# A gated long convolution and a gated feed-forward on one core: four homes in on-chip memory, the first half's output stage inside the second half's spectra, and the feed-forward's opening in another order

## The chip, the core and the metric

One NeuronCore of one Trainium2 chip. The five engines that the text names are TensorE (PE in the profile, with its weight loads as PEld), VectorE (DVE), ScalarE (ACT), GpSimd (POOL) and SyncE (SP), which here only issues transfers. The time is device microseconds of one execution. A program whose time is compared is run several times and its median is taken.

## What is computed

A block with adaptive layer norm, over 2048 rows of 448 channels, all in float32:

```python
mod = silu(c) @ w_mod                       # six vectors of 448: sa, ca, ga, sb, cb, gb
h = layernorm(x) * (1 + ca) + sa            # x is q
kv = causal_conv4(k, shift_k) * v           # per channel, 4 taps
y = irfft(rfft(kv, 4096) * rfft(ssm_k, 4096))[:2048] + kv * ssm_D
x = x + ga * h * y
h = layernorm(x) * (1 + cb) + sb
x = x + gb * ((sigmoid(h @ w_gate) * (h @ w_up)) @ w_down)     # 448 -> 1792 -> 448
```

## The kernel before

**Layout.** A tile has 128 partitions. The 2048 rows are 16 groups of 128. The 448 channels are two halves of 224 (`h` = 0 and 1 in names such as `y0_3`, `av[:, h]`, `gate(h, i)`).

**The convolution** is done by Fourier transforms written as matmuls. `stage1_k` and `stage1_v` (lines 171 and 183) do a first small transform, the VectorE transposes 32 by 32 blocks in place (`turn`, line 167: eight turns for a half), `stage2_k` and `stage2_v` (229 and 259) do the second. `stage2_v(h, between)` runs eight steps `n`. Each step multiplies on PE into an accumulator `s2v`, multiplies that on the VectorE by the kernel's spectrum `ak` and by its copy with swapped halves `kx` (which a transfer `load_kx` brings, two buffers), and transforms the two products `m` back on PE (`inv`, into `sa`), from where ACT copies them over the spectrum in `av`. `inv` runs one step late. After it `between(n)` emits whatever else is to stand there. When a half's eight steps and its eight turns are done, `stage_out(h, i)` (299) makes output rows of four groups, eight matmuls per `i` into an accumulator `y`, `y_copy` brings it out of PSUM, and `gate(h, i, y, eng)` (314) multiplies with the first norm's result `G` and adds to the residual `x1`. The half 0 is gated on POOL, half 1 on the VectorE. The six modulation vectors are made on the way: a transfer `mod_load`, three POOL instructions `mod_sum`, a PE sum over partitions `mod_use`.

**The feed-forward** holds each float32 operand as a high and a low part, and multiplies high x high, low x high and high x low. Its 1792 hidden columns are 7 groups of 256 (`j`), the rows 4 blocks of 512 (`n`), so there are 28 blocks `(j, n)`, each with two halves `f`. `gate_up(j, n, f)` (630) is 22 matmuls: 11 for the gate (`s` = 0), 11 for the up product (`s` = 1), into one `gu` accumulator, of which there are two. ACT and VectorE make the hidden values `hh` and `hl` from it. `down(j, n, hs, e)` (651) is 12 matmuls into an accumulator `d`, and the VectorE adds `d` to `x1`. The down product of a block is emitted during the next block: after `gate_up(.., 0)` comes `down(*prev, 0)`, after `gate_up(.., 1)` comes `down(*prev, 1)`. A weight group `j` arrives by six transfers of raw weights `r` (`load_w(j, k)`: k = 0, 1 gate, 2, 3 up, 4, 5 down), and `split_hi` (ACT) and `split_lo` (VectorE) make the two parts in `wt`; the down weights are first multiplied by `gb` on POOL.

**The second norm** of a block of rows: statistics (`ln2_stats`, two of four row groups on ACT with `sq`, the others on the VectorE), `ln2_end` (square root on ACT, reciprocal on VectorE), `norm_rows(n)` (601, the VectorE writes normed rows `xn`), `norm_turn(n, t)` (611, four PE transposes into `pt`, ACT and VectorE make the high and low parts in `xt`).

**What sets the order.** Nothing is scheduled by a tool: `tc.manual_schedule()` (450) keeps the order in which the Python emits, and each engine runs its own list in that order. Waits follow from the tiles: an instruction waits for the writers of what it reads, and a tile that takes a place in memory waits for the readers of the tile that was there. Around the change the order is set by `during0` and `during1` (548 and 563, the `between` of the two halves), by the lines 577 to 683, and by the tables `jobs` and `ends` (708 to 727): `jobs[p, f]` is emitted inside `gate_up` of block number `p`, `ends[p, f]` behind the down product. Blocks 0 to 7 are `(0,0), (1,0), (0,1), (1,1), (0,2), (0,3), (1,2), (1,3)`. All transfers below are issued by SP in order.

**Places in memory.** Pool `big` has the tags `ak` (two buffers: the kernel's spectra of both halves, later the weights `wt` of two groups) and `av` (one buffer: the spectra of `kv` of both halves, later `xt`). Raw weights have two buffers of their own (`pr`, line 426).

## Time and profile before

| | us |
|---|---|
| median of 3 executions | 667.43 (665.19 to 670.30) |
| the profiled execution | 668.59 |
| its span, first to last instruction | 666.8 |
| last matmul of the second half's spectra ends, about | 177 |
| last turn of the second half ends, about | 187 |
| first feed-forward matmul | 208.14 |
| from here on PE has no gap | 300.26 |

How to read it: the page gives each engine's busy time and the span in 40 slices of 16.7 us. A timeline row is start, duration, engine, line, operation, tiles, shape, and in brackets the idle time of that engine before it with what ended it. Durations overlap at their ends where an engine is pipelined, so the time from one start to the next is the price of an instruction in a row of them. `x8` at the end of a row is a count of merged instructions; a float32 matmul shows as two.

### The profile page before, as it was taken

What the parts mean: (1) busy time and instruction counts of PE and PEld (TensorE: products, weight loads), DVE (VectorE), ACT (ScalarE), POOL (GpSimd) and SP (SyncE); (2) the same over time, 40 slices, a digit from 0 to 9 for tenths busy, and PEclk for the clock granted to TensorE, in tenths of its full rate; (3) what the DMA queues carried; (4) which work ended last, traced back from release to release, by engine and by line L of the source; (5) the groups of instructions that cost most, each with busy time, mean ns of one, the idle gap of its engine ahead of it and who ended that gap; (6) DMA issues with size and microseconds to landing.
All of it is one profiled execution on the core that took longest, in us unless ns stands there. A gap on an engine that the chain in (4) does not pass through costs nothing.

```text
span 666.8 us, 7048 instructions
## 1 busy us (share of the span) xinstructions
PE 597.1 (90%) x2764; PEld 457.5 (69%) x2764; DVE 350.1 (53%) x402; ACT 251.1 (38%) x436; POOL 131.5 (20%) x101
## 2 busy tenths in 40 slices
PE   8597795998847677789999999999999999999997
PEld 6355442433435366678888888888888888888886
DVE  0859985989998644433224443344334433442233
ACT  5575577974535476341113222222212212221110
POOL 1224286689890100000001001000000100000000
PEclk9898997999986789899999999999999999999999
DMA  8931288773210200000001111001101010100112
GB/s 296 282 83 54 82 293 206 190 183 88 68 46 15 90 32 1 0 1 0 1 1 59 32 32 43 17 16 30 46 1 32 28 32 16 31 15 0 56 55 111
DMA packets 23765, 44.44 MB, mean 67 GB/s; under 512 B 10354, under 2 KB 12916, under 8 KB 23604
## 3 DMA queue, kind: packets, MB, share of 16 engines
q1 hardware_dynamic: 23668, 43.98, 23.0%
q8 instruction: 22, 0.36, 0.2%
q14 instruction: 11, 0.09, 0.0%
q0 software_dynamic: 64, 0.01, 0.0%
HBM read 32.98 MB, written 3.67 MB: 55 GB/s over the span
## 4 chain that ended last, share of the span: by engine, by line
PE 65%; DVE 13%; DMA 8%; ACT 7%; issue 3%; POOL 3%; SPq 0%; POOLq 0%; DVEq 0%; ACTq 0%
PE gu L639 39%; PE d L662 20%; DVE av L169 4%; PE s2k L234 3%; DVE acc L208 2%; DMA kT<-in_kT_dram 2%; DMA wm<-in_wmod_dram 2%; PE pt L618 2%; POOL wm L333 1%; ACT full L620 1%; DMA early<-in_ssm_dram 1%; DVE wt L443 1%; POOL wm L334 1%; DMA r<-in_wu_dram 1%; ACT xt L624 1%
## 5 line engine op out<-in xcount | busy, mean ns | idle before, releaser
L639 PE MATMUL gu<-xt,wt 128*128 128x512 f32 x1232 | 299.1, 398 | 3.6 <-ACT wt L437 3.6
L639 PEld LDWEIGHTS gu<-xt,wt 128*128 128x128 f32 x1232 | 236.2, 192 | 52.2 <-ACT wt L437 4.0
L644 DVE TENSOR_TENSOR sg<-sg,gu 128x512 f32<-128x512 f32 x56 | 38.4, 686 | 198.8 <-ACT sg L643 198.8
L662 PE MATMUL d<-wt,hh 128*128 128x448 f32 x448 | 127.4, 366 | 1.9 <-ACT sq L372 1.9
L643 ACT ACTIVATE sg<-gu 128x512 f32<-128x512 f32 x56 | 33.4, 597 | 252.5 <-PE gu L639 252.5
L662 PEld LDWEIGHTS d<-wt,hh 128*128 128x128 f32 x448 | 84.0, 188 | 11.9 <-ACT sq L372 2.4
L436 POOL TENSOR_TENSOR r<-r,gbrow 128x448 f32<-128x448 f32 x14 | 16.0, 1147 | 374.1 <-DMA r<-in_wd_dram 339.6
L662 PE MATMUL d<-wt,hl 128*128 128x448 f32 x224 | 81.8, 365 | 0.0
L663 DVE TENSOR_TENSOR x<-x,d 128x896 f32<-128x896 f32 x56 | 60.5, 1081 | 2.4 <-PE d L662 2.4
L648 DVE TENSOR_TENSOR hl<-sg,hh 128x512 fp32r<-128x512 f32 x56 | 39.7, 708 | 39.1 <-ACT hh L647 39.1
L169 DVE STREAM_TRANSPOSE av<-av 128x896 f32<-128x896 f32 x32 | 57.8, 1875 | 2.4 <-POOL wm L335 2.4
L647 ACT ACTIVATE hh<-sg 128x512 fp32r<-128x512 f32 x56 | 35.4, 631 | 45.3 <-DVE sg L644 45.3
L662 PEld LDWEIGHTS d<-wt,hl 128*128 128x128 f32 x224 | 42.1, 188 | 3.3
L618 PE MATMUL pt<-ident,xn 128*128 128x128 f32 x64 | 13.9, 336 | 22.8 <-ACT xt L624 10.5
L443 DVE TENSOR_TENSOR wt<-r,wt 128x512 fp32r<-128x512 f32 (+1 forms) x42 | 32.5, 789 | 2.8 <-ACT wt L437 2.8
L169 DVE STREAM_TRANSPOSE ak<-ak 128x896 f32<-128x896 f32 x16 | 28.1, 1815 | 9.7 <-ACT ak L181 9.7
L234 PE MATMUL s2k<-ak,w 128*128 128x448 f32 x64 | 27.1, 578 | 6.7 <-ACT acc L206 6.5
L274 PE MATMUL sa<-m,wa 128*64 128x448 f32 x64 | 28.0, 553 | 5.3 <-ACT av L276 3.4
L288 PE MATMUL s2v<-av,w 128*128 128x448 f32 x64 | 28.8, 576 | 1.7 <-ACT ak L235 1.7
L618 PEld LDWEIGHTS pt<-ident,xn 128*128 128x128 f32 x64 | 8.5, 162 | 29.0 <-ACT xt L624 11.8
L437 ACT ACTIVATE wt<-r 128x512 fp32r<-128x512 f32 (+1 forms) x42 | 24.7, 600 | 9.4 <-DMA r<-in_wu_dram 9.4
L275 PE MATMUL sa<-m,wa 128*64 128x448 f32 x64 | 27.5, 552 | 0.0
(121 smaller groups left out, 569.4 us busy)
## 6 DMA issues: line engine op xcount, KB each, us to landing
kx<-ak SPq DMA_DIRECT2D x32, 224.0 KB, 4.1
wm<-in_wmod_dram SPq DMA_DIRECT2D x12, 392.0 KB, 4.4
v<-in_v_dram SPq DMA_DIRECT2D x8, 448.0 KB, 9.1
x<-in_q_dram SPq DMA_DIRECT2D x4, 896.0 KB, 9.5
r<-in_wg_dram SPq DMA_DIRECT2D x14, 256.0 KB, 2.7
r<-in_wu_dram SPq DMA_DIRECT2D x14, 256.0 KB, 2.7
out_dram<-x SPq DMA_DIRECT2D x8, 448.0 KB, 2.5
r<-in_wd_dram SPq DMA_DIRECT2D x14, 224.0 KB, 2.5
```

Of the source, the lines that this page charges most:

```text
L169: DVE.transpose(x, x)
L234: PE.matmul(pt[:, b, :D], w2, a[:, j + 2 * b:j + 2 * b + 2], start=True, stop=True)
L288: PE.matmul(pt[:, b, :D], w2, a[:, j + b * nj // 2:j + (b + 1) * nj // 2, cs], start=True, stop=True)
L443: DVE.tensor_sub(lo, r, hi)
L618: PE.transpose(pt[:, i * P:(i + 1) * P], xn[:, i, t * P:(t + 1) * P], ident)
L639: PE.matmul(pgu[:, s], w[:, t, f * P:(f + 1) * P], x[:, xs], start=i == 0, stop=i == len(ops) - 1)
L643: ACT.activation(sg, pgu[:, 0], AF.Sigmoid)
L644: DVE.tensor_mul(sg, sg, pgu[:, 1])
L647: ACT.activation(hh, sg, AF.Copy)
L648: DVE.tensor_sub(hl, sg, hh)
L662: PE.matmul(pt[:, i, :D], h[:, (2 * e + i) * P:(2 * e + i + 1) * P], w[:, f], start=m == 0, stop=m == len(ops) - 1)
L663: DVE.tensor_add(x1[:, g:g + 2], x1[:, g:g + 2], rows(pt))
```

## The change

**Places.** `big` now has four tags with one buffer each. `k0` and `k1` hold the kernel's spectra of the halves, `a0` and `a1` those of `kv`. Later `k0` holds `tmp` (16 x 224 columns for copies of `y`, and seven places of 512 columns for raw weights), then rows 2 and 3 of the norm's result (`xt1`); `a0` holds `xt0` (rows 0 and 1); `k1` and `a1` hold the weights of even and odd groups. Later raw weights use the four `in` buffers. `stage1_v` copies each accumulator out with two ACT instructions of 448 elements, one for each half, where it was one of 896.

**Second half's spectra.** `during1` has the raw weights of group 0 loaded (three at n = 5, three at n = 6) and, at n = 5, 6, 7, `stage_out(0, 0..2)` with copy and gates; `(0, 3)` follows behind. The last two `mod_sum` stand in `during0`, their `mod_use` at n = 0 and 1. Raw weights 0 to 5 of group 0 need no buffer to come free.

**Feed-forward's opening.** Groups 0 and 1 have their raw weights in `tmp`. Only one of four statistics is on ACT for the first two row blocks. `norm_rows(n)` for n > 0 is on ACT. `norm_turn` does eight transposes at once, and the copies (`norm_split`) are separate. The norm work that stood in `jobs` is spread by `turns` and a new `ends`. `down` always uses the accumulator `y` (it alternated between `sa` and `y`); norm turns of n > 0 use `sa`.

```diff
 def stage1_v(k):
-            ACT.activation(d[:, :, g], rows(pt).rearrange("p s (h c) -> p s h c", h=2), AF.Copy)
+            for h in range(2):
+                ACT.activation(av[h].rearrange("p (s j) c -> p s j c", s=2)[:, :, g], pt[:, :, h * C:h * C + C], AF.Copy)
...
 def during0(n):
+        if n in (4, 5):
+            mod_sum(n + 6)
...
+    tmp = big.tile([P, 32 * C], F32, tag="k0", name="tmp")
 def during1(n):
-        if n < 2:
-            mod_sum(n + 10)
         if n < 5:
             next(gating)
-        if n in (3, 5):
-            mod_use(10 + n // 4)
+        if n < 2:
+            mod_use(10 + n)
...
+        if n in (5, 6):
+            for k in range(3):
+                load_raw(0, 3 * (n - 5) + k, raw(3 * (n - 5) + k))
+        if n >= 5:
+            gate(0, n - 5, y_copy(0, n - 5, stage_out(0, n - 5, "y")), POOL)
...
-    for k in range(2):
-        load_w(0, k)
-    for i in range(4):
-        if i < 3:
-            turn(av[:, 1], 2 * i + 2)
-            turn(av[:, 1], 2 * i + 3)
-        if i > 1:
-            split_hi(0, i - 2)
-        gate(0, i, y_copy(0, i, stage_out(0, i, "sa" if i % 2 else "y")), POOL)
-    y1 = [stage_out(1, i, tag) for i, tag in ((0, "y"), (1, "t"), (2, "t"))]
-    for k in range(2):
-        split_lo(0, k)
-        load_w(0, 2 + k)
-        split_hi(0, 2 + k)
+    for i in range(3):
+        turn(av[1], 2 * i + 2)
+        turn(av[1], 2 * i + 3)
+        if i == 0:
+            gate(0, 3, y_copy(0, 3, stage_out(0, 3, "y")), POOL)
+    new_w(0)
+    for k in range(4):
+        split_hi(0, k)
+    y1 = [stage_out(1, i, tag) for i, tag in enumerate(("sa", "t", "t", "y"))]
+    for k in range(3):
+        split_lo(0, k)
     gate(1, 0, y1[0], DVE)
...
-        pt = two("y" if e else "sa", f"d{j}_{g}")
+        pt = two("y", f"d{j}_{g}")
...
-    ln2_stats(0, 1, 2, 3, act=(0, 1))
-    yc = y_copy(1, 1, y1[1])
-    for k in (2, 3):
-        split_lo(0, k)
-        load_w(0, 2 + k)
-    ln2_end(0)
+    yc = [y_copy(1, 1, y1[1])]
+    ln2_stats(0, 1, 2, 3, act=(0,))
+    ln2_end(0, 1)
+    new_w(1)
+    split_lo(0, 3)
+    for k, at in enumerate((6, 0, 1, 2)):
+        load_raw(1, k, raw(at))
+    yc += [y_copy(1, i, y1[i]) for i in (2, 3)]
     norm_rows(0)
-    for t in range(4):
-        norm_turn(0, t)
...
+    norm_turn(0, 0, "sa")
+    norm_turn(0, 2, "y")
+    norm_split(0, 0)
+    norm_split(0, 2)
+    gate(1, 1, yc[0], DVE)
+    ln2_stats(4, 5, 6, 7, act=(4,))
+    for k in range(2):
+        split_w(1, k)
+    ln2_end(4, 1)
...
+    turns = {(1, 1, 0): (1, 0), (1, 1, 1): (1, 2), (2, 1, 0): (2, 0), (3, 0, 0): (2, 2), (3, 1, 0): (3, 0), (4, 0, 0): (3, 2)}
+    ends = {(0, 0): [splits_of(1, 2, 3), splits_of(0, 4, 5)],
+            (0, 1): [lambda: norm_rows(1), lambda: gate(1, 2, yc[1], DVE)],
+            (1, 0): [lambda: gate(1, 3, yc[2], DVE), lambda: load_raw(1, 4, raw(0)), lambda: load_raw(1, 5, raw(6))],
+            (1, 1): [stats_of(2), splits_of(1, 4, 5), lambda: xts.append(big.tile([P, 2, 7, 512], F32R, tag="k0", name="xt1"))],
+            (2, 0): [lambda: norm_rows(2)],
+            (2, 1): [stats_of(3)],
+            (3, 0): [lambda: norm_rows(3)],
```

**How rows move, first place:** PE's list in the last steps of the second half's spectra. `s2v1_6` is the forward product of step 6, `sa1_5` an inverse product of step 5, `y0_0` the first output product of half 0. Before:

```order
L288 MATMUL s2v1_6_1152<-av_276,w2_76 128x448 x2
L274 MATMUL sa1_5_1159<-m1_5_0_1136,wa_84 64x448
...
L288 MATMUL s2v1_7_1166<-av_276,w2_76 128x448 x2
L274 MATMUL sa1_6_1173<-m1_6_0_1155,wa_84 64x448
...
L275 MATMUL sa1_7_1180<-m1_7_1_1170,wa_84 64x448
L306 MATMUL y0_0_1200<-av_276,wb_85 64x224 x8
L306 MATMUL y0_1_1215<-av_276,wb_85 64x224 x8
```

Now:

```order
L305 MATMUL y0_0_1170<-av0_276,wb_85 64x224 x8
L287 MATMUL s2v1_6_1185<-av1_277,w2_76 128x448 x2
L273 MATMUL sa1_5_1192<-m1_5_0_1157,wa_84 64x448
...
L305 MATMUL y0_1_1202<-av0_276,wb_85 64x224 x8
L287 MATMUL s2v1_7_1214<-av1_277,w2_76 128x448 x2
L273 MATMUL sa1_6_1221<-m1_6_0_1188,wa_84 64x448
...
L305 MATMUL y0_2_1228<-av0_276,wb_85 64x224 x8
```

Three groups of eight output products now stand ahead of forward and inverse products of the other half: `y0_0` ahead of `s2v1_6`, `y0_1` ahead of `s2v1_7`, `y0_2` ahead of `sa1_7`.

**Second place:** ACT's list where it makes the high part `wt1` of group 1's down weights. `sg` and `hh` are hidden values, `full` and `xt` the norm's parts, `sq` statistics, `rstd` the square roots. Before, in block 1, `(1, 0)`:

```order
L381 ACTIVATE rstd_91<-mv_93,eps_82 128x2 x2
L643 ACT_TABLE_LOAD
L643 ACTIVATE sg1_0_0_1553<-gu1_0_0_1497 128x512
L647 ACTIVATE hh1_0_0_1556<-sg1_0_0_1553 128x512
L437 ACTIVATE wt1_1403<-r1_4_1467 128x448
L437 ACTIVATE wt1_1403<-r1_5_1471 128x448
```

Now, at the end of block 1 and the start of block 2, `(0, 1)`:

```order
L635 ACTIVATE full1_3_1585<-pt1_2_1572,cols_89 128x512
L639 ACTIVATE xt0_1318<-pt1_2_1572,cols_89 128x512
L657 ACTIVATE sg1_0_1_1589<-gu1_0_1_1532 128x512
L661 ACTIVATE hh1_0_1_1592<-sg1_0_1_1589 128x512
L371 ACTIVATE sq8_1610,mv_93<-x1_701 128x448
...
L372 ACTIVATE sq9_1613,mv_93<-x1_701,mv_93 128x448
L381 ACT_TABLE_LOAD
L381 ACTIVATE rstd_91<-mv_93,eps_82 128x2 x2
L440 ACTIVATE wt1_1336<-tmp_1027 128x448 x2
L657 ACT_TABLE_LOAD
L657 ACTIVATE sg0_1_0_1656<-gu0_1_0_1633 128x512
```

The high part of group 1's down weights stands behind four statistics, a table load and two square roots; the first product that reads it is `down(1, 0, .., 0)`, at the end of the first half of block 2. Before, it stood right behind `hh1_0_0`, a whole half-block earlier.

More of the change, by code (lines that the diff above doesn't have):

```diff
@@ L103, in quad @@
     def quad(tag, bufs, name, parts=P):
-        return (rot if tag == "in" else late["rb"]).tile([parts, 4, C], F32, tag=tag, bufs=bufs, name=name)
+        return (rot if tag == "in" else late["pg"] if tag == "G" else late["rb"]).tile([parts, 4, C], F32, tag=tag, bufs=bufs, name=name)
     def whole(t):
@@ L484, in adaln_conv_glu_kernel @@
         load_k(ct, kb)
-    av = big.tile([P, 2, 32, C], F32, tag="av", name="av")
+    av = [big.tile([P, 32, C], F32, tag=f"a{h}", name=f"av{h}") for h in range(2)]
     for k in range(4):
@@ L548, in during0 @@
     def during0(n):
-        turn(av[:, 1], n)
+        turn(av[1], n)
         if n < 5:
@@ L691, in stats_of @@
         return run
-    def turns_of(n, t0, tag):
-        def run():
-            for t in range(t0, t0 + 2):
-                norm_turn(n, t, tag)
-        return run
     def splits_of(j, *ks):
```

136 lines of the change are left out of this document (63 added, 73 removed).

## Prediction

> **What bounds the kernel now.** I read the page's slices first, then windows by stage, then the chain and the timelines.
>
> ```profile
> span 666.8 us, 7048 instructions
> PE   8597795998847677789999999999999999999997
> 190.00:210.00 20.00, 11.63 (x67) 8.53 (x64) 16.71 (x24) 9.10 (x18) 10.66 (x6) 0.67 0.17 48
> 230.00:250.00 20.00, 14.06 (x55) 10.67 (x55) 10.58 (x20) 13.67 (x25) 2.22 (x2) 0.83 0.14 47
> 350.00:660.00 310.00, 310.00 (x1422) 266.61 (x1421) 117.53 (x157) 66.72 (x114) 11.50 (x10) 1.00 0.10 31
> 300.43 5.00 PE gu L639 x22
> 305.43 2.43 PE d L662 x12
> 307.86 5.00 PE gu L639 x22
> 292.75 0.45 PE pt L618 x4
> 208.14 12.09 PE L639 MATMUL gu<-xt,wt 128*128 128x512 f32 x44
> 223.79 5.44 PE L639 MATMUL gu<-xt,wt 128*128 128x512 f32 x11 [3.56 <-ACT wt L437]
> ```
>
> In a window the columns are length, then busy time of PE, PE's weight loads, VectorE, ACT and POOL, the granted clock, the share and rate of the transfers. From 350 to 660 PE is busy without a gap at clock 1.00, and it has been since 300.26: a half-block costs 5.00 + 2.43 = 7.43 us. That stretch can't change, so the end comes earlier by as much as PE gets there earlier. In 190 to 250 PE is neither full nor at full clock. By 300.26 PE has done 8 gate-and-up halves, 6 down halves and 12 groups of four norm transposes: 8 x 5.00 + 6 x 2.43 + 12 x 0.45 = 60.0 us of work in 300.26 - 208.14 = 92.1 us. So the opening loses 32.1 us. The two things to forecast are when the first product starts, and what the opening loses now.
>
> **Second half's spectra.** Here the VectorE sets the pace, row behind row.
>
> ```profile
> 163.59 3.71 DVE L169 STREAM_TRANSPOSE av<-av 128x896 f32<-128x896 f32 x2
> 169.06 1.18 DVE L290 TENSOR_TENSOR m<-s2v,ak 128x896 f32<-128x896 f32 x1
> 174.75 12.21 DVE L169 STREAM_TRANSPOSE av<-av 128x896 f32<-128x896 f32 x7
> 165.92 1.67 PE L288 MATMUL s2v<-av,w 128*128 128x448 f32 x4
> 176.93 6.22 PE L306 MATMUL y<-av,wb 128*64 128x224 f32 x64
> ```
>
> The change adds a wait. `y0_0` needs all turns of half 0, done at 163.59 + 3.71 = 167.3. Behind it on PE stands `s2v1_6`, which started at 165.92, and the VectorE waits for that. Eight output products cost 6.22 / 4 = 1.55, the forward product 1.7: `s2v1_6` ends at 170.6, and the VectorE's product of step 6 starts there and not at 169.06, +1.5. Then come inverse products (1.5), `y0_1` (1.55) and `s2v1_7` (1.7), to 175.3, while the VectorE is ready at 170.6 + 2.0 + 12.21/7 = 174.3: another +1.0. So the last turn ends at 189.5, where it ended at 187.0. Bounds: 0 if PE fits the products into gaps; +5 if the last `kx`, now queued on SP behind three raw loads, comes late.
>
> **Gates on POOL.**
>
> ```profile
> 136.11 2.11 POOL L408 TENSOR_TENSOR G<-G,arow 128x896 f32<-128x896 f32 x1 [2.08 <-ACT G L407]
> 156.68 1.68 POOL L333 TENSOR_TENSOR wm<-wm,sc 112x896 f32<-112x896 f32 x1
> 160.29 2.10 POOL L408 TENSOR_TENSOR G<-G,arow 128x896 f32<-128x896 f32 x1
> 175.19 2.12 POOL L409 TENSOR_TENSOR G<-G,brow 128x896 f32<-128x896 f32 x1
> 196.15 2.41 POOL L319 TENSOR_TENSOR x<-x,G 128x896 f32<-128x896 f32 x1
> 186.79 4.44 DVE L443 TENSOR_TENSOR wt<-r,wt 128x512 fp32r<-128x512 f32 x2
> 223.86 1.29 DVE L443 TENSOR_TENSOR wt<-r,wt 128x512 fp32r<-128x512 f32 x2
> 199.43 2.51 DVE L605 TENSOR_SCALAR xn<-x,rstd,nmr 128x448 f32<-128x448 f32 x4
> 229.19 1.78 DVE L605 TENSOR_SCALAR xn<-x,rstd,nmr 128x448 f32<-128x448 f32 x4
> 232.59 1.54 DVE L648 TENSOR_TENSOR hl<-sg,hh 128x512 fp32r<-128x512 f32 x1 [0.70 <-ACT hh L647]
> 191.27 2.71 DMA r<-in_wu_dram
> ```
>
> A modulation sum is 3.6 us (156.68 to 160.29). Two stood among the `G` instructions; one of them now fits into POOL's idle time before the norm, the other delays the first `G` by 1.5. Eight `G` at about 4.2 then end at 171.6 (before 177.3), and four gates of 4.2 at about 188.5, the last when its copy allows; before they ended at 198.6. That matters for the VectorE: two weight subtractions took 4.44 beside POOL and 1.29 alone, four `xn` 2.51 and 1.78. I count 3.2 + 0.7 won. The scaling of two down weights on POOL now falls at 188.5 to 190.8 and costs back about 0.8 (the slowed `hl` of 1.54). The wait of 2.71 for raw up weights goes too: they are loaded 10 us before use.
>
> **From the last turn to the end of block 0.**
>
> ```profile
> 187.11 7.96 PE L306 MATMUL y<-av,wb 128*64 128x224 f32 x64 [3.95 <-ACT yc L311]
> 188.00:190.00 2.00, 2.00 (x16) 0.54 0.12 17
> 222.00:224.00 2.00, 0.21 (x1) 0.57 0.00 0
> 207.35 0.43 DVE L622 CAST xt<-full 128x512 fp32r<-128x512 f32 x1 [0.88 <-ACT full L620]
> 207.81 0.69 DVE L626 TENSOR_TENSOR xt<-full,xt 128x512 fp32r<-128x512 f32 x1
> 236.44 0.54 ACT L371 ACTIVATE sq<-x 128x448 f32<-128x448 f32 x1
> 239.40 1.28 ACT L381 ACT_TABLE_LOAD   x1
> ```
>
> (Two windows of PE alone: length, busy, clock, transfers.) After holes of 3.95 and 3.56 us the clock shows 0.54 and 0.57, and it stays near half for some 4 us. With most output products moved forward PE now idles from about 181.4 to 189.6, so the first of `y1` run at half clock: 3.1 each for two of them, about 1.5 us late in all.
>
> The steps: last turn 189.5; three weight subtractions at 0.65 + 0.8 for POOL, 192.2; first `y1` 192.7; its gate, two instructions of 1.1, 194.9; statistics of four row groups, of which ACT has one (half of 239.40 - 236.44, 1.5, behind the copy of the late `y1_1`), root, reciprocal and one subtraction, 199.3; four `xn` 1.78, 201.1; transposes, copy, first cast, first product at 202.8. The four parts need 0.43 + 0.69 each on the VectorE, so the last is ready at 206.7; 11 gate products end at 207.2, the first 22 at 209.7, the second 22 at 214.7. Before, they ended at 208.14 + 12.09 = 220.2. **First gain: 5.5 us.** Bounds: 0 (cold clock through the first 22, late `kx`) and 9 (no later turns).
>
> **Opening, blocks 1 to 4.** Before, from 220.2 to 300.26 PE had 60.0 - 10.0 = 50.0 us of work in 80.0, so 30.0 lost. The stall of 3.56 goes, with its cold 11 products (5.44, warm 2.5): group 1's first weights need nothing but `tmp`, and are split before the first sigmoid. The stalls at every norm turn, which waited for one accumulator that ACT had to empty twice, mostly go, because eight transposes come at once and the copies run beside 11 products. What I find left:
>
> ```profile
> 263.85 0.67 PE L662 MATMUL d<-wt,hh 128*128 128x448 f32 x2 [1.93 <-ACT sq L372]
> 136.74 1.96 ACT L407 ACTIVATE G<-x,nmr,rstd 128x224 f32<-128x224 f32 x4
> 246.95 0.78 ACT L620 ACTIVATE full<-pt,cols 128x512 f32<-128x512 f32 x1 [1.54 <-PE pt L618]
> ```
>
> First, the down product of block 1 now waits for ACT. PE reaches it at 214.7 + 3 x 5.0 + 2 x 2.43 + 4 x 0.45 + 0.4 for a wait on the accumulator = 236.8. ACT: four `xn`, now here, at an estimated 0.63 each (0.49 for half the elements in `G`, 0.78 for 512 in `full`) until 222.3; the third `full` waits until the VectorE has done two gates, a hidden value, an addition and a subtraction, 230.4; four copies at 0.7, 233.2; hidden value 2.0; two row groups' statistics 2.96, table load 1.28, roots 0.5, then the weights' high part 0.5 and low part 0.6: 241.0. A wait of 4.0 (before, a like row waited 1.93). After a hole of 3.6 I expect a clock drop, as the 3.56 hole gave: 1.9 more. [...] Second, `xn` of row block 3 stands late on ACT, 1.9. Third, 0.4 at the accumulator of the turns, 0.4 for slower `xn`, 1.0 for POOL's two scalings beside four subtractions. Together 9.6. **Second gain: 30.0 - 9.6 = 20.4.** Bounds: 3 lost (ACT keeps pace) and 20 lost (most old waits return).
>
> **Small terms.**
>
> ```profile
> 659.69 1.09 DVE L663 TENSOR_TENSOR x<-x,d 128x896 f32<-128x896 f32 x1 [1.10 <-PE d L662]
> 85.66 1.73 ACT L193 ACTIVATE av<-s1v 128x896 f32<-128x896 f32 x2 [0.31 <-PE s1v L192]
> 94.14 0.35 ACT L350 ACTIVATE brow<-mod 128x224 f32<-128x224 f32 x1
> ```
>
> With one accumulator for all down products the last one must wait for the addition of the one before: 1.09 + 0.25 = 1.35 lost at the end. Elsewhere 5.00 us of gate-and-up products lie between two down products and hide the addition; each that came more than 3.5 us late would cost its excess. The 16 split copies: 0.35 for 224 and 0.92 for 896 elements give about 0.54 for 448; the pair ends 0.05 later than the one, a few times on PE's path, 0.2. Bounds 0 and 1.5. Memory places and the earlier sums cost nothing: POOL and SP idle there.
>
> **Sum** against the profiled execution, 668.59 with its span of 666.8 (1.8 around it): -5.5 - 20.4 + 1.35 + 0.2 = -24.3, span 642.5, time 644.3. The median of the runs shown, 667.43, is 1.2 lower, so I forecast a median of **643.0 us**, 3.7% less.
>
> **Rivals.**
> - *ACT keeps pace.* The wait at block 1's down product and the cold clock fall away, because ACT reaches the weights four microseconds earlier than my chain says. For it: ACT is half idle in 230 to 250 (13.67 of 20). Against it: the row of 263.85 shows this very kind of wait. 643.0 - 7 = 636.
> - *The first half of the change gives nothing, or the places in memory bring new waits* (it doesn't do what it says). The turns end later, PE is cold, block 0 ends at 220 as before, and the opening still loses 15: 643.0 + 5.5 + 5.4 = 654. For it: the VectorE bounds the spectra and gets no instruction less there. Against: POOL no longer slows it behind the last turn.
> - *The clock stays down (slower than before).* Place: the opening. If its holes come so close that PE never gets the 4 us of unbroken work after which the clock rose at 212, ten halves, eight down halves and the turns run at 0.5: 74.8 us of work take 150, and block 4 ends at 352 instead of 315 before: 667.4 + 37 + 1.5 = 706. Each microsecond of work done cold costs one more; from 24 of them on nothing is left of the gain, from 31 the change is slower by 1%. For it: 0.67 and 0.83 above. Against: the longest stretches of unbroken work are now 7.4 us or more. [...]
>
> **Chances.** My sum 0.50 (its own range 638 to 649), ACT keeps pace 0.20, little from the first half 0.20, cold opening 0.04, other 0.06. The range reaches from the first rival's 633 to the second's 657. About 1% (6.7 us) is what a measurement of this kernel can tell from no change. Faster by more than that: 0.90; within 1%: 0.06 (the second rival's tail); slower: 0.04.
>
> **What would show it.** Right: the last turn near 189.5 with two VectorE gaps of 1 to 1.5 in steps 6 and 7; PE empty 181 to 189 and its clock near 0.5 at 190; first product at 202 to 204; no wait for raw weights in block 1; one wait of about 4 at the first down product of block 2, released by ACT or the VectorE; steady half-blocks of 7.43 from about 288; 1.3 before the last down product. Wrong: a first product after 206, PE waits of more than 10 us in all between 215 and 288, or a steady half-block above 7.5.

## The result and the profile after

The changed kernel takes 647.56 us in the median of four executions (643.83 to 648.36), beside 668.87 for the kernel before on the same chip. The ratio is 0.9678, with a 95% interval of 0.9619 to 0.9737: 3.2% faster. The forecast was 643.0, from 633 to 657.

From the changed kernel's page, the span and PE's slices:

```profile
span 645.2 us, 7056 instructions
PE   7596895999848989999999999999999999999995
```

Its window over the stretch of the opening that the prediction showed of before (length, busy time of PE, weight loads, VectorE, ACT, POOL, granted clock, transfers):

```profile
230.00:250.00 20.00, 16.05 (x70) 12.75 (x69) 12.86 (x22) 15.54 (x28) 0.00 (x0) 0.91 0.05 14
```

In 230 to 250 PE has 16.05 busy at clock 0.91 where it had 14.06 at 0.83, and VectorE and ACT have more to do in the same 20 us (12.86 and 15.54 for 10.58 and 13.67): the program is further on. The rows that the prediction named, from the changed kernel's timelines, first up to the first feed-forward product:

```profile
170.69 1.09 DVE L289 TENSOR_TENSOR m<-s2v,ak 128x896 f32<-128x896 f32 x1 [1.58 <-PE s2v L287]
175.56 1.09 DVE L289 TENSOR_TENSOR m<-s2v,ak 128x896 f32<-128x896 f32 x1 [0.96 <-PE s2v L287]
177.57 12.21 DVE L168 STREAM_TRANSPOSE av<-av 128x896 f32<-128x896 f32 x7
189.69 2.53 DVE L446 TENSOR_TENSOR wt<-tmp,wt 128x512 fp32r<-128x512 f32 x3
189.92 8.95 PE L305 MATMUL y<-av,wb 128*64 128x224 f32 x64 [8.21 <-DVE av L168]
193.29 1.09 DVE L318 TENSOR_TENSOR G<-G,y 128x896 f32<-128x896 f32 x1 [1.07 <-PE y L305]
203.57 3.35 PE L654 MATMUL gu<-xt,wt 128*128 128x512 f32 x9
```

Both waits for `s2v` are there, the last turn ends at 177.57 + 12.21 = 189.8, PE has its hole ahead of it. The first product starts at 203.57. Then PE in the opening:

```profile
243.00 1.40 PE L676 MATMUL d<-wt,hh 128*128 128x448 f32 x2 [3.25 <-ACT wt L440]
247.33 2.69 PE L654 MATMUL gu<-xt,wt 128*128 128x512 f32 x11
282.88 5.16 PE L654 MATMUL gu<-xt,wt 128*128 128x512 f32 x22
290.32 5.16 PE L654 MATMUL gu<-xt,wt 128*128 128x512 f32 x22
```

One long wait stands at the first down product of block 2, and from 282.88 PE runs in half-blocks of 290.32 - 282.88 = 7.44. The end, VectorE's last additions:

```profile
630.70 0.69 DVE L658 TENSOR_TENSOR sg<-sg,gu 128x512 f32<-128x512 f32 x1 [4.35 <-ACT sg L657]
632.71 1.08 DVE L677 TENSOR_TENSOR x<-x,d 128x896 f32<-128x896 f32 x1
636.68 1.09 DVE L677 TENSOR_TENSOR x<-x,d 128x896 f32<-128x896 f32 x1 [2.90 <-PE d L676]
640.57 1.09 DVE L677 TENSOR_TENSOR x<-x,d 128x896 f32<-128x896 f32 x1 [2.80 <-PE d L676]
```

These three come 3.97 and 3.89 apart. The first and the last of the three before, which had stood at 657.51, 659.69 and 662.12, so 2.18 and 2.43 apart:

```profile
657.51 1.08 DVE L663 TENSOR_TENSOR x<-x,d 128x896 f32<-128x896 f32 x1
662.12 1.09 DVE L663 TENSOR_TENSOR x<-x,d 128x896 f32<-128x896 f32 x1 [1.34 <-PE d L662]
```

To compare executions, the span is cut at four rows that every kernel has: the end of the first half's last turns (the rows `av` x2 near 163), the first `gu` product, VectorE's last `sg` product, its last addition. The stretch ahead of the first cut ends between 165.2 and 168.2 in the runs below without any edit of it, so those 3 us are not an edit's doing; the three stretches behind it are what is compared. The columns are in us, of one profiled execution each; median and ratio are of the timed ones. The kernels were timed on several chips, each beside runs of the kernel before on the same chip, whose median lay between 667.61 and 669.46; the ratio is to those runs, so it need not follow the medians. The executions of one kernel spread over 1.5 to 7 us. A difference of a microsecond or two between two medians therefore tells little by itself; such prices are read from the rows and the stretches.

| kernel | turns to first product | first product to last `sg` | last `sg` to last addition | median | ratio to before |
|---|---|---|---|---|---|
| before | 40.84 | 447.38 | 6.60 | 668.87 | |
| the change | 36.41 | 427.13 | 9.87 | 647.56 | 0.9678 |
| end_two_homes | 36.29 | 427.17 | 6.60 | 644.98 | 0.9673 |
| weights_first | 36.21 | 427.69 | 9.86 | 647.80 | 0.9701 |
| weights_first_turns_late | 36.15 | 421.83 | 9.84 | 640.54 | 0.9600 |
| out_one_step_later | 36.66 | 426.95 | 9.84 | 646.86 | 0.9693 |
| out_after_turns | 38.45 | 427.41 | 9.81 | 648.39 | 0.9703 |
| turns_one_by_one | 36.32 | 438.65 | 9.85 | 654.96 | 0.9810 |
| group1_weights_late | 36.27 | 429.27 | 9.85 | 648.47 | 0.9693 |
| turns_share_accumulators | 36.26 | 430.84 | 6.61 | 647.10 | 0.9689 |
| gates_ahead | 36.42 | 430.28 | 9.88 | 649.39 | 0.9711 |
| opening_four_undone | 36.57 | 441.31 | 6.60 | 657.48 | 0.9830 |
| end_and_turns_late | 36.36 | 421.82 | 6.61 | 636.66 | 0.9524 |
| end_turns_late_warm | 35.23 | 421.43 | 6.60 | 635.80 | 0.9516 |

So the change won 4.4 in the first stretch and 20.25 in the second, and lost 3.27 in the third; 0.14 was won ahead of them and 0.05 behind: 21.6, the difference of the spans.

### The profile page after: what moved, and what is told of

Same layout as the page of the kernel before. It is cut to its first block, busy times and chain, and to the rows that moved or that the text cites. A ratio compares the mean times of both kernels' runs of the same rounds, so it can differ in the third digit from the quotient of the medians.

```text
span 645.2 us, 7056 instructions
## 1 busy us (share of the span) xinstructions
PE 589.9 (91%) x2764; PEld 451.7 (70%) x2764; DVE 340.1 (53%) x394; ACT 255.3 (40%) x456; POOL 130.0 (20%) x101
## 4 chain that ended last, share of the span: by engine, by line
PE 65%; DVE 14%; ACT 8%; POOL 4%; issue 4%; DMA 3%; SPq 1%; DVEq 0%; POOLq 0%; ACTq 0%
PE gu L654 38%; PE d L676 20%; DVE av L168 3%; DVE acc L207 2%; DVE ak L168 2%; PE s2k L233 2%; DMA wm<-in_wmod_dram 2%; POOL wm L333 2%; PE y L305 1%; POOL wm L334 1%; PE s1v L190 1%; ACT xn L615 1%; DVE v L226 1%; PE s2v L287 1%; ACT full L635 1%
## 5 line engine op out<-in xcount | busy, mean ns | idle before, releaser
L654 PE MATMUL gu<-xt,wt 128*128 128x512 f32 x1232 | 292.0, 391 | 0.6 <-DVE xt L643 0.6
L654 PEld LDWEIGHTS gu<-xt,wt 128*128 128x128 f32 x1232 | 231.2, 188 | 48.0 <-DVE xt L643 1.1
L676 PE MATMUL d<-wt,hh 128*128 128x448 f32 x448 | 129.2, 369 | 6.5 <-ACT wt L440 3.3
L439 POOL TENSOR_TENSOR r<-r,gbrow 128x448 f32<-128x448 f32 x10 | 11.5, 1156 | 318.9 <-DMA r<-in_wd_dram 312.6
L233 PEld LDWEIGHTS s2k<-ak,w 128*128 128x128 f32 x64 | 13.0, 206 | 19.2 <-issue 9.3
L207 DVE SCALAR_TENSOR_TENSOR acc<-kT,sk,acc 112x512 f32<-112x512 f32 x24 | 21.9, 921 | 8.6 <-ACT acc L205 8.1
L209 POOL TENSOR_TENSOR acc<-kT,sk 112x512 f32<-112x512 f32 x16 | 18.8, 1202 | 37.1 <-PE kv0y L220 15.3
L305 PE MATMUL y<-av,wb 128*64 128x224 f32 x128 | 15.7, 405 | 9.9 <-DVE av L168 9.9
## 6 DMA issues: line engine op xcount, KB each, us to landing
kT<-in_kT_dram SPq DMA_DIRECT2D x4, 616.0 KB, 12.6
```

The costliest lines, as they stand in the source:

```text
L207: DVE.scalar_tensor_tensor(a, x, w, a, op0=OP.mult, op1=OP.add)
L233: PE.matmul(pt[:, b, :D], w2, a[:, j + 2 * b:j + 2 * b + 2], start=True, stop=True)
L654: PE.matmul(pgu[:, s], w[:, t, f * P:(f + 1) * P], x[:, xs], start=i == 0, stop=i == len(ops) - 1)
L676: PE.matmul(pt[:, i, :D], h[:, (2 * e + i) * P:(2 * e + i + 1) * P], w[:, f], start=m == 0, stop=m == len(ops) - 1)
```

## Experiments

Theory: the time comes and goes at the places that the prediction names, each with a price of its own. The rivals are that a wait which is removed only moves, that the first half of the change gives nothing, and that one part of the opening hides what another costs. All edits are made to the changed kernel.

### Four parts that could be better

**end_two_homes**

```diff
-        pt = two("y", f"d{j}_{g}")
+        pt = two("sa" if j > 1 and e == 0 else "y", f"d{j}_{g}")
```

> Edit: from weight group 2 on, the down products alternate between two accumulators again; nothing else. The changed kernel (span 645.2, median 647.6) has at its end VectorE additions 3.89 us apart (632.71, 636.68, 640.57), before they were 2.43 apart. Theory: the end costs two waits of 1.46 us plus 0.35 of fill, 3.3 in all, so the span becomes 641.9 and the median 644.3, and the steady period of 7.43 is unchanged. Rival (the term of the prediction): only one wait, 1.35, so span 643.9 and median 646.2. Second rival: the additions are also behind something in the steady stretch; then its period falls below 7.43 and more than 4 us are won.

VectorE's last rows in this kernel:

```profile
633.40 1.09 DVE L677 TENSOR_TENSOR x<-x,d 128x896 f32<-128x896 f32 x1 [1.10 <-PE d L676]
635.83 1.09 DVE L677 TENSOR_TENSOR x<-x,d 128x896 f32<-128x896 f32 x1 [1.34 <-PE d L676]
```

They are 2.43 apart again, as before the change. From the last `sg` to the last addition it is 6.60, 3.27 less, and the stretch ahead of it is unchanged (427.17 for 427.13). The theory holds, 3.27 for the expected 3.3: the program ends with three down products in a row, so two of them wait for an addition, not one. The median is 2.6 lower, the ratio only 0.0005; that the end gains is read from the rows.

**weights_first and weights_first_turns_late**

```diff
-            (1, 1): [stats_of(2), splits_of(1, 4, 5), ...
+            (1, 1): [splits_of(1, 4, 5), stats_of(2), ...
```

and in the second also

```diff
-    turns = {..., (2, 1, 0): (2, 0), (3, 0, 0): (2, 2), (3, 1, 0): (3, 0), (4, 0, 0): (3, 2)}
+    turns = {..., (3, 0, 0): (2, 0), (3, 1, 0): (2, 2), (4, 0, 0): (3, 0), (4, 1, 0): (3, 2)}
```

> Edit: after block 1's second half the two down weights of group 1 are split ahead of the statistics of row block 2, not behind them. Theory A (the wait is the price): the 3.25 us at the first down product of block 2 and the 1.9 us of cold clock behind it go, span 645.2 - 5.1 = 640.1, median 642.4. Theory B (ACT is the bound there, the wait is only where it shows): ACT works without a gap from 237.2 to 249.3 in either order, so the normalised row block 2 is ready at 249.3 as before; PE passes the down product at 239.8 and stands at the norm turn from 244.9 to 249.3 instead. A hole of 4.4 with its cold clock, gain 0 to 0.8, span about 644.8, median 647.2.

> Edit: the same, and the four norm turns of row blocks 2 and 3 stand one half-block later (they were needed only at blocks 4 and 5). Theory B: PE has 7.4 us more of other work ahead of the turn, so the hole closes and ACT catches up: the wait of 3.25, its cold clock of 1.9 and the three waits of 0.33 for row block 3 go; span 645.2 - 6.1 = 639.1, median 641.4. Theory A: the same gain as with the weights alone, 640.1, and nothing for the turns. Third possibility: ACT stays behind by the same amount to the end of block 4; then a wait of 3 or more shows up at blocks 4 or 5, which need the turns' parts, and the span is above 643.

The timeline of weights_first, PE and ACT around block 2:

```profile
239.44 0.92 PE L676 MATMUL d<-wt,hh 128*128 128x448 f32 x2
246.36 2.70 ACT L615 ACTIVATE xn<-x,nmr,rstd 128x448 f32<-128x448 f32 x4
247.16 0.33 PE L627 MATMUL pt<-ident,xn 128*128 128x128 f32 x1 [2.26 <-ACT xn L615]
249.75 4.25 PE L654 MATMUL gu<-xt,wt 128*128 128x512 f32 x11
```

The down product now starts without a wait. The transposes behind it wait instead, and the 11 products after them take 4.25 for 2.69: by that length the cold clock moved along, an estimate from the kernel before, where 11 such products took 5.44 at a clock of 0.50. The reason is the second row. ACT writes `xn` of row block 2 at 246.36; in the changed kernel that row is at 246.61. ACT has the same list to do in either order, and 647.80 is no gain on 647.56. Theory B holds. With the turns half a block later PE has other work in that stretch, and the two waits that are left there are

```profile
247.02 0.68 PE L676 MATMUL d<-wt,hh 128*128 128x448 f32 x2 [0.85 <-DVE x L677]
252.63 1.09 PE L627 MATMUL pt<-ident,xn 128*128 128x128 f32 x8 [0.42 <-ACT sq L372]
```

The second stretch is 5.3 shorter than in the changed kernel, the median 7.0 lower; 6.1 was expected. Beside weights_first, on the same chip, all four executions are faster (640.12 to 641.88 for 646.05 to 648.59). What the late turns would give without the weights first no run shows.

**out_one_step_later**

```diff
-        if n >= 5:
-            gate(0, n - 5, y_copy(0, n - 5, stage_out(0, n - 5, "y")), POOL)
+        if n >= 6:
+            gate(0, n - 6, y_copy(0, n - 6, stage_out(0, n - 6, "y")), POOL)
...
-        if i == 0:
-            gate(0, 3, y_copy(0, 3, stage_out(0, 3, "y")), POOL)
+        if i < 2:
+            gate(0, 2 + i, y_copy(0, 2 + i, stage_out(0, 2 + i, "y")), POOL)
```

> Edit: the first half's four output products stand one step later each (behind the forward products of steps 6 and 7 and two of the turns). Theory (the prediction's): the two waits of VectorE on the forward products, 1.58 and 0.96, go; the last turn ends at about 187.4 instead of 189.8, first product 2.2 earlier at 201.4, span 643.0, median 645.4. Rival: those waits cost nothing, because PE, its clock or POOL's gates bind behind the turns anyway; first product 203.6 as now, span 645.2. The hole of PE ahead of the second half's output shrinks from 8.2 to about 5; if the clock then stays up, the output of the second half takes 6.3 instead of 8.95.

Its timeline, VectorE, POOL and PE:

```profile
172.22 1.09 DVE L289 TENSOR_TENSOR m<-s2v,ak 128x896 f32<-128x896 f32 x1 [1.27 <-PE s2v L287]
186.23 5.37 DVE L446 TENSOR_TENSOR wt<-tmp,wt 128x512 fp32r<-128x512 f32 x3
187.09 2.40 POOL L319 TENSOR_TENSOR x<-x,G 128x896 f32<-128x896 f32 x1
```

Only one of the two waits went, so the last turn ends at 186.4, 21.15 behind the first half's turns where it was 22.62: 1.5 won. But the three weight subtractions now meet POOL's last gate and its scalings, and take 5.37 for 2.53: 2.8 lost. PE had less of a hole (5.33 for 8.21), and its output products took 7.95 for 8.95. In sum the first product comes 36.66 behind the turns, for 36.41: the rival holds. The span, 643.4, is near the theory's 643.0 only because the stretch ahead of the first cut was 1.9 shorter, which is not the edit's doing. The waits that the prediction counted are real, but removing them in this way is worth nothing: POOL's last gate then ends later (189.5 for 188.3), the VectorE's subtractions start earlier, and the two meet.

### Parts of the change undone

**out_after_turns**

```diff
-        if n >= 5:
-            gate(0, n - 5, y_copy(0, n - 5, stage_out(0, n - 5, "y")), POOL)
...
-    for i in range(3):
-        turn(av[1], 2 * i + 2)
-        turn(av[1], 2 * i + 3)
-        if i == 0:
-            gate(0, 3, y_copy(0, 3, stage_out(0, 3, "y")), POOL)
+    for i in range(4):
+        if i < 3:
+            turn(av[1], 2 * i + 2)
+            turn(av[1], 2 * i + 3)
+        gate(0, i, y_copy(0, i, stage_out(0, i, "sa" if i % 2 else "y")), POOL)
```

> Edit: the first half's output products, their copies and their gates go back behind the second half's turns, as in the kernel before; raw weights, sums of the modulation and the whole opening stay as changed. Theory (early output is what brings the first gain of 4.5 us): the last turn ends about 2.4 earlier than now (22.5 us behind the last half-0 turns become 20), but then 64 more output products (6.2), their copies and four gates of 4.2 on POOL stand between it and the norm; POOL's gates run to about 204 beside the VectorE's subtractions and statistics, so the first product comes 2 to 5 later than the 203.57 of now, span 647 to 650, median 650 to 652. Rival (the early output gives nothing; the first gain is that of the early raw weights and sums): first product 201.5 to 203.6, span 643 to 645.

Its timeline:

```profile
185.34 6.98 DVE L446 TENSOR_TENSOR wt<-tmp,wt 128x512 fp32r<-128x512 f32 x3
186.73 2.53 POOL L318 TENSOR_TENSOR G<-G,tmp 128x896 f32<-128x896 f32 x1
185.73 6.28 PE L305 MATMUL y<-av,wb 128*64 128x224 f32 x64 [3.98 <-DVE av L168]
195.30 0.63 DVE L375 BATCH_NORM_STATS2 st<-x 128x6 f32<-128x448 f32 x1
204.33 3.35 PE L652 MATMUL gu<-xt,wt 128*128 128x512 f32 x9
```

The last turn ends at 185.6, 19.7 behind the first half's turns and 2.9 earlier than in the changed kernel, and PE's hole is halved (3.98). The output products behind it take 6.28 and not 8.95. At clock 1.00 they took 6.27 (end_turns_late_warm), so by their length this hole did not cool the clock. The three subtractions, now beside POOL's gates all along, take 6.98, and the first product comes 2.0 later, counted from the first half's turns. In the median it is 0.8. So the early output gives 2.0 of the 4.4 us of the first stretch: not by the VectorE's turns, which it delays, but because POOL is done before the VectorE's last work begins.

**turns_one_by_one, group1_weights_late, turns_share_accumulators, gates_ahead**

The four edits in this order, one kernel each (in the first, `norm_split` also gets a third argument, the parts that it copies):

```diff
-                    norm_turn(*turns[p, f, s])
-                    norm_split(*turns[p, f, s])
+                    n_, t0 = turns[p, f, s]
+                    pt = two("sa", f"pt{n_}_{t0}")
+                    for t in (t0, t0 + 1):
+                        for i in range(4):
+                            PE.transpose(pt[:, t - t0, i * P:(i + 1) * P], xns[n_][:, i, t * P:(t + 1) * P], ident)
+                        xps[n_, t0] = pt
+                        norm_split(n_, t0, (t,))
```

```diff
-    for k, at in enumerate((6, 0, 1, 2)):
-        load_raw(1, k, raw(at))
...
-    for k in range(2):
-        split_w(1, k)
+    for k in range(4, 6):
+        split_w(0, k)
+    for k in range(2):
+        load_raw(1, k, raw(4 + k))
...
-    ends = {(0, 0): [splits_of(1, 2, 3), splits_of(0, 4, 5)],
+    ends = {(0, 0): [splits_of(1, 0, 1), lambda: load_raw(1, 2, raw(4)), lambda: load_raw(1, 3, raw(5))],
...
+                if (p, f, s) == (0, 1, 0):
+                    splits_of(1, 2, 3)()
```

```diff
-        pt = two("y", f"d{j}_{g}")
+        pt = two("y" if e else "sa", f"d{j}_{g}")
...
-                    norm_turn(*turns[p, f, s])
+                    norm_turn(*turns[p, f, s], "sa" if f else "y")
```

```diff
-    gate(1, 1, yc[0], DVE)
+    for i in range(1, 4):
+        gate(1, i, yc[i - 1], DVE)
...
-            (0, 1): [lambda: norm_rows(1), lambda: gate(1, 2, yc[1], DVE)],
-            (1, 0): [lambda: gate(1, 3, yc[2], DVE), lambda: load_raw ...
+            (0, 1): [lambda: norm_rows(1)],
+            (1, 0): [lambda: load_raw ...
```

> Edit: in the six norm turns of row blocks 1 to 3 the four transposes of the second part stand behind the copies of the first again (in the same accumulator), not ahead of them. Theory (this was most of the opening's stalls): PE waits about 1.6 at each of six turns for the two copies, 9.6 in all, less what the wait of 3.25 at the down product takes back where ACT sets the pace; span 645.2 + 7 to 10 = 652 to 655, median 655 to 657. Rival: the copies are off the path, since ACT is the bound in the opening whichever way they stand; span below 648.

> Edit: the raw weights of group 1 are loaded only when the down weights of group 0 have been split, into their two places, and pass in two pairs, so they come about 20 us later, as before the change. Theory A (the prediction's): the early loads removed the stall of 3.56 and its cold clock, 2.9; they come back, +6.5, span 651.7, median 654. Theory B: the transfers of 0.9 us each were not what was late, but ACT and VectorE, which split the weights behind statistics and a root; with those rearranged PE waits 0.7 for the first and about 1 for the second pair, +1.5 to 3, span 646.7 to 648.2, median 649.5.

> Edit: down products alternate between both accumulators everywhere and the turns use whichever was used last, as in the kernel before; eight transposes still come at once. Theory: the end wins 3.3, as shown; in the opening the first turn of block 2 waits for the VectorE's addition, which stands behind two gate instructions and ends at 230.1 where the turn comes at 226.9, +3.2, with up to 2 of cold clock; the other five turns come after their addition and lose nothing. Span 645.2 - 3.3 + 3.2 to 5.2 = 645 to 647. Rival 1: the wait is absorbed by the 3.25 of the down product two steps on, span 642. Rival 2: every turn waits as before the change (1.5 each), span above 650.

> Edit: the second half's gates 2 and 3 go back to where they stood before the change, ahead of row block 1's statistics; in the changed kernel they stand in the opening's blocks. Four VectorE instructions of 1.09 us change place, nothing else. Theory (the order of VectorE's and ACT's work is what is left of the second gain): statistics, group 1's weight split and the first sigmoid come 4.4 us later; PE waits about 1.4 and 2 for group 1's weights in block 1 and 1 for the hidden value, with up to 3 of cold clock, and gets 1 to 2 back at the turns of row block 1: span 645.2 + 3 to 8 = 648 to 653, median 650 to 655. Rival: the VectorE has the same work in either order and the later wait at the down product takes the difference up; span within 1 of 645.2, median 647 to 648.5.

PE's waits in the opening, of turns_one_by_one (total, times, longest), and one row of its timeline:

```profile
PE pt L750 <- ACT xt L639: 11.0, 6, 2.5
```

```profile
267.64 4.36 PE L654 MATMUL gu<-xt,wt 128*128 128x512 f32 x11
```

Six waits of 1.5 to 2.5, the down product's wait down from 3.25 to 1.3, and, by their length, products at a cold clock behind three of the waits (4.35, 4.10 and 4.36 for 2.7; 11 such products took 5.44 at clock 0.50 in the kernel before). The median is 7.4 higher, at the lower end of what was expected; the profiled execution was the longest of the four (658.76, the others 653.55 to 655.11), so its rows show the price too high.

The same view of group1_weights_late, turns_share_accumulators and gates_ahead:

```profile
PE gu L654 <- ACT wt L440: 1.4, 2, 0.8
```

```profile
PE pt L627 <- DVE x L677: 4.7, 2, 3.2
```

```profile
PE gu L654 <- DVE sg L658: 3.4, 1, 3.4
```

Late raw weights, with the splits set around them, cost 1.4 of waiting for ACT's part and 0.5 for VectorE's, 2.1 in the stretch and 0.9 in the median: theory B in the span (647.4), 1.0 under its median. Nor were the transfers what made the 3.56 of the kernel before: its raw gate weights were issued from 217.61 on and land 2.7 to 2.8 us after their issue, and ACT came to them only at 223.12, straight behind a table load and two hidden-value instructions. Shared accumulators cost the expected 3.2 at one turn, 1.5 at another, which was not expected, and win 3.27 at the end, -0.5 in the median. The gates ahead cost 3.4 at the third set of gate and up products: there are two `gu` accumulators, and the VectorE's first `sg` row, which frees one, now stands behind four gate instructions. The theory had expected waits for group 1's weights and the hidden value instead. The median is 1.8 higher, below the theory's 650 to 655 and outside the rival's 647 to 648.5; that the price is real is read from the row and the stretch (3.15 longer).

**opening_four_undone** has these four edits together.

> Edit: four parts of the new opening undone together: turns one by one, accumulators shared, group 1's weights late, gates 2 and 3 ahead. Alone they moved the median from 647.6 by +7.4, -0.5, +0.9 and +1.8. Theory A (each has its own price): the sum, +9.6, median 657.2. Theory B (each is partly hidden by the others' arrangement: one queue that comes late is made up for by another that is early, and several together leave no slack and cool the clock): +13 to +17, median 661 to 665, most of the 21 between the two kernels. Theory C (the same wait is counted in several of them): below +8, median under 655.6.

The median is 657.48, 9.9 above the changed kernel; the four medians alone add up to 9.6. That is where theory A put it, and theory B's 661 to 665 did not come. That no part hides what another costs is not shown, though: by the spans of the profiled executions, one each, the four add up to 11.8 + 2.2 - 0.6 + 2.7 = 16.1 and make 12.6 together, and the waits have changed hands. The turns' 4.7 for the VectorE's addition and the 3.4 at the accumulators are gone, and the 1.4 at the weights has become 4.6. Of the waits in its opening these two are the largest,

```profile
PE pt L753 <- ACT xt L639: 10.4, 6, 2.7
PE gu L654 <- ACT wt L440: 4.6, 1, 4.6
```

and these are the largest of the kernel before, in the same view:

```profile
PE pt L618 <- ACT xt L624: 10.5, 6, 2.6
PE gu L639 <- ACT wt L437: 3.6, 1, 3.6
PE pt L618 <- DVE x L663: 3.1, 2, 1.6
PE d L662 <- ACT sq L372: 1.9, 1, 1.9
```

The two kinds of stall that led the old opening are back, at about the old size. With the end left out the four parts make 9.9 + 3.27 = 13.2 by the median, and 441.31 - 427.13 = 14.2 by the stretch, of the 20.25 won in the opening. The other 6 to 7 were not taken apart: what is left of the change there is where the turns stand, how the statistics are shared out, the norm's rows on ACT and block 0's eight transposes at once. The old waits for the VectorE's addition (3.1) and for the squares (1.9), which do not come back with the four, point to the first two of these; that is argued, not shown.

### A faster version

**end_and_turns_late** joins end_two_homes with weights_first_turns_late; **end_turns_late_warm** adds to it

```diff
+    pt = two("y", "warm2")
+    for i in range(30):
+        PE.matmul(pt[:, 0, :P], ones, ones, start=True, stop=True)
     new_w(0)
...
+    pt = two("t", "warm3")
+    for i in range(14):
+        PE.matmul(pt[:, 0, :P], ones, ones, start=True, stop=True)
     norm_turn(0, 0, "sa")
     norm_turn(0, 2, "y")
+    for i in range(5):
+        PE.matmul(pt[:, 0, :P], ones, ones, start=True, stop=True)
```

> Edit: the two edits that won, together: two accumulators for the down products from weight group 2 on, and the down weights of group 1 ahead of the statistics with the turns of row blocks 2 and 3 a half-block later. Theory: they are far apart (end, opening) and add up: 645.2 - 3.3 - 6.1 = 635.8 for the span, median 637.5. Rival: the down products of the opening still share one accumulator, and the wait of 0.85 seen there grows; span above 637.

> Edit: the same, and products of ones with ones into a free accumulator, read by nobody, keep PE busy in its holes: 30 ahead of the second half's output products, 14 ahead of the first transposes, 5 behind them. Theory A (the prediction charged about 1.5 for the cold clock there): the granted clock stays at 1.00 from 180 to 206, the first output product ends about 1.6 earlier, VectorE's wait for it (0.7 to 1.7 in the runs so far) goes, first product 1 earlier, span 1 below that of the kernel without them. Theory B: VectorE's chain, 2.5 of weight subtractions and then the gate, takes the place of the wait, so less than 0.5 is won. Theory C: the added products push the output products back, slower by 1 or more.

The two gains add up: 636.66, span 635.4 (expected 637.5 and 635.8). Against the kernel before that is a ratio of 0.9524, from 0.9479 to 0.9569. With the added products the timeline and the clock window read

```profile
181.61 6.97 PE L596 MATMUL warm<-ones 128*128 128x128 f32 x60 [1.02 <-ACT tmp L311]
188.88 6.27 PE L305 MATMUL y<-av,wb 128*64 128x224 f32 x64 [0.31 <-DVE av L168]
201.28 2.94 PE L657 MATMUL gu<-xt,wt 128*128 128x512 f32 x9
```

```profile
186.00:188.00 2.00, 2.00 (x21) 1.00 0.00 0
```

and without them

```profile
188.71 8.94 PE L305 MATMUL y<-av,wb 128*64 128x224 f32 x64 [8.18 <-DVE av L168]
192.07 1.09 DVE L318 TENSOR_TENSOR G<-G,y 128x896 f32<-128x896 f32 x1 [1.03 <-PE y L305]
202.35 3.36 PE L654 MATMUL gu<-xt,wt 128*128 128x512 f32 x9
```

```profile
186.00:188.00 2.00, 0.00 (x0) 0.50 0.00 0
```

The clock stays at 1.00, the output products take 6.27 for 8.94, the VectorE's wait goes, and the first product comes 1.1 earlier behind the turns: theory A. In the median it is 0.9 (635.80), which the intervals (0.9470 to 0.9561 beside 0.9479 to 0.9569) do not tell apart from nothing; the rows do.

## Why the prediction was right, and where it was off

The forecast of faster was right and the time lies in the range, also in the likeliest case's own (638 to 649). The median came 4.6 above the 643.0: 2.7 from the sum, 1.2 from the step to a median 1.2 below the profiled execution, while this one came 0.5 above its own, and 0.1 of rounding.

- **Bound.** Right. PE is full from 282.88, at the old period, up to the last two down products. The prediction wrote about 288; its own sums put this half-block at 300.26 - 25.9 + 7.43 + 0.9 = 282.7.
- **Second half's spectra.** Right in size: waits of 1.5 and 1.0 forecast, 1.58 and 0.96 measured; last turn at 189.5 forecast, 189.8 measured; POOL's gates end at 188.5 forecast, 188.3 measured. That the waits are a loss that could be had back was not shown to be so (out_one_step_later).
- **First gain, 5.5 forecast, 4.4 measured.** The first product was forecast for 202.8 and came at 203.57. Two small steps were too short. The gate of `y1` began at 193.29 and not at 192.7: the last turn was 0.3 late and the cold output product (clock 0.50 from 190 to 195) took the rest. And from the row of `xn` to the first product it takes 3.9 (199.64 to 203.57), where the prediction left 3.5. The cold clock was charged at about its size: in end_turns_late_warm, without it (1.00 from 180 to 210), the first stretch is 1.1 shorter and the second 0.4, in all 1.5. The prediction had put its 1.5 on the output products alone.
- **Second gain, 20.4 forecast, 20.25 measured.** The wait at the down product was 3.25 (4.0 forecast), and the clock drop behind it (0.50 from 244 to 246) 247.33 - 243.00 - 2.43 = 1.9, as forecast. The prediction took that drop from the hole of 3.56 in the kernel before; in out_after_turns a hole of 3.98 brought none, by the 6.28 of the products behind it, so that it came true is in part luck. The waits for `xn` of row block 3 made 1.0 where 1.9 was forecast, and waits of 0.66 at a turn and 0.51 at a hidden value were not on the list. The sum was met because such misses cancel. That the turns' stalls would go because eight transposes come at once is shown (7.4). That the weights' stall would go because they need nothing but `tmp` was the wrong half of the reason: late weights cost 0.9 in the median and 2.1 in the stretch, and what mattered was also what stood ahead of them on VectorE and ACT (the wait at them was 1.4 with late weights alone, 4.6 with the other three edits as well).
- **End, 1.35 forecast, 3.27 measured.** This is the term that was mis-sized most, 1.9 of the 2.7. The prediction counted the last down product. The kernel ends with three, the previous block's second and the last block's two, because a block's down product comes a block late. Two wait: the spaces between the additions are 3.97 and 3.89, and were 659.69 - 657.51 = 2.18 and 2.43.
- **Small term.** The split copies were charged 0.2; the stretch that they lie in is 0.14 shorter, which its spread of 3 us does not tell from nothing.
- **Rivals.** *ACT keeps pace* was priced as if the wait at the weights were the cost, and it called ACT half idle in 230 to 250, where 13.67 of 20 were busy. weights_first takes that wait away and nothing is won: the rival asks for less work on ACT ahead of `xn`, or more on PE, and an order that gives that (turns half a block later) was worth 7.0 in the median and 5.3 in the stretch, about what the rival had said. *The first half gives nothing* did not come: the first stretch is 4.4 shorter. The early output gives 2.0 of it; where the other 2.4 come from no run shows. *The clock stays down* did not come: between 180 and 283 the clock fell to 0.50 three times, from 186 to 195, from 203 to 205 and from 244 to 246, and was back at 1.00 from 196, 206 and 247 on.

## What to carry to other kernels

A wait in a profile names the instruction that came last, not the engine that has too much to do: look whether the engine that releases it works without a gap behind that point too, and if so give the waiting engine other work instead of moving the awaited instruction ahead. When two tiles are merged into one, count the places where its users come in a row without other work between them, at the end of the program above all, where a pipeline drains. Work moved to an earlier time on GpSimd was worth here what it no longer held up on the VectorE (three subtractions took 2.53, and 6.98 in out_after_turns), more than what its own end says.

## What the runs showed of the hardware

Three VectorE subtractions of 128x512, with both operands in on-chip memory, took 2.53 at the end of POOL's scalings, 5.37 beside a gate's second half and the scalings, and 6.98 beside gates all along: up to 2.3 each, for the 0.65 that the prediction took from before. The other side can lose as well. In gates_ahead they meet POOL's two scalings, and it is the scalings that are slow:

```profile
188.92 2.10 DVE L446 TENSOR_TENSOR wt<-tmp,wt 128x512 fp32r<-128x512 f32 x3
187.88 4.14 POOL L439 TENSOR_TENSOR tmp<-tmp,gbrow 128x448 f32<-128x448 f32 x2
```

In the changed kernel those took 2.25. In gates_ahead the subtractions started at 188.92, just ahead of the second scaling, and that scaling took about 3.04: it started at about 188.98, an estimate from 187.88 and the 1.10 between the two starts in the changed kernel. In the changed kernel the second scaling had started at 189.3, ahead of the subtractions at 189.69, and these took the longer. In both, by these starts, the engine that came second gave way; two cases make no rule. A statistics row, with one input, took 0.63 in out_after_turns (195.30) and 0.63 in gates_ahead (195.09). In gates_ahead POOL's last row had ended at 192.02; in out_after_turns it had work to 197.8 at least, an estimate from its row at 186.73, three more gate instructions of 2.10 and the scalings' 2.25.

The clock fell in two ways. In the changed kernel PE is empty from 181.7, the window from 184 to 185 has 1.00, that from 185 to 186 has 0.57 and the next 0.50: a fall 3.3 to 4.3 us into the hole. In out_one_step_later it came later: PE is empty from 181.1, the window from 184 to 186 has 1.00 and that from 186 to 188 has 0.63, a fall 4.9 us or more after PE went empty. In out_after_turns a hole of 3.98 brought none, by the 6.28 of the products behind it. In the kernel before it came earlier: PE is empty from 220.23, the window from 221 to 222 has 1.00 and that from 222 to 223 has 0.64, a fall after 1.8 to 2.8 us. So no one length of a hole fits these four. And in the changed kernel the clock fell again where the hole was shorter than any of them:

```profile
200.00:201.00 1.00, 0.60 (x2) 1.00 0.00 0
201.00:202.00 1.00, 0.85 (x6) 1.00 0.00 0
202.00:203.00 1.00, 1.00 (x8) 0.60 0.00 0
```

These are windows of one microsecond of the changed kernel's PE (length, busy, clock, transfers). A hole of 1.49 ahead of the transposes, and short waits among these (0.85 busy from 201 to 202), were all the idle time that PE had between 190 and this fall; in end_turns_late_warm, with added products around the transposes, the clock stayed at 1.00 (194 to 206). Whether short holes add up or transposes count for less than other products no run here tells.
